# Weight forms made in a staggered order from two rings, loads ahead of stores, one normalisation piece a step

## The chip, the cores and the metric

The kernel runs on one core of a Trainium2 chip, in one launch. The metric is the device time of a run in microseconds. A core has TensorE (matmuls), VectorE, ScalarE, GpSimd, and SyncE, whose queue issues nearly all DMAs here; each engine takes its instructions in the order in which the program lists them.

## What is computed

Attention over a window of 64 positions, then a feed-forward layer with an ELU, then eight experts whose outputs are all added with gate weights that come from eight rounds of row and column normalisation:

```python
attn = softmax(q @ k^T / 8 within the window) @ v        # 4 x 8 heads x 576 x 64
x = attn as (2304, 512)
h = x @ w_in;  x = elu(h) @ w_out                        # d_ff 2048
P = exp(x @ w_gate - max)
for _ in range(8):
    P /= P.sum(1) + 1e-9;  P /= P.sum(0) + 1e-9;  P *= N / E
out = sum over e of P[:, e] * (relu(x @ w1[e]) @ w2[e])  # E 8, F 1024
```

All is float32. Products are made of three passes with operands split into a high part (rounded to the matmul format) and a low part (the rest): high x high, high x low, low x high.

## The kernel before

The stages run one after another, each keeping TensorE fed: attention with the first quarter of the feed-forward layer mixed in; the other quarters (`steps`, 20 steps each for five token blocks and four hidden chunks; four blocks of 512 tokens and one of 256); the experts for the first 768 tokens by plain products (`esteps`); the experts for the other 1536 tokens by a transformed product with seven half-size products for eight.

The seven products need sums and differences of quarters of `w1[e]` and `w2[e]`. These *forms* are made once, while the plain products of `esteps` run, and written to DRAM. There are 64 pieces, `h` = 0 to 63: expert, one of four 128-row groups, and `w1` (even) or `w2` (odd). A piece has four raw blocks of 128 x 256 and four sums of them, in eight slots. `p_tasks(h)` lists five tasks for a piece: `sums1` and `sums2` (two sums each, GpSimd), `high` (ScalarE rounds all eight slots into the tile `f`, line 666), `low` of slots 0 to 3 (VectorE, line 670), and `rest`, which makes `low` of slots 4 to 7, issues the store of seven slots and then, through `p_load(h + 2)`, four loads of 128 KB (lines 630, 635). The raw tile `rw` has eight slots and two buffers; tile `f` has eight buffers, of which 0 and 1 are in pool A1, 2 and 3 in A2 (opened at step 2 of `esteps`), 4 to 7 in B, which takes the place of the pool big1 once the gates' products are done (`done2`).

Who makes which task when is written out by hand. In the last 20 steps of the feed-forward layer the loads of pieces 0 and 1 go out at step 2, and from step 9 on each step takes one task off `ptasks`. In `esteps` each step s first lists the first product of a chunk (`e_in`), then the second product of the chunk two steps back (`e_out`), then up to two pieces of `extra`, then tasks until `ntask` reaches a goal that grows by 5 tasks for every 3 clock units (a clock unit is 256 tokens of a chunk):

```python
            clock += nb[j] // 256
            goal = 5.0 * (4.0 + clock / 3.0)
            if s >= 2:
                lim = 5 * (NHU if done2 else 4)
                while ptasks and ntask < min(goal, lim):
```

A unit of the loop is two or four chunks over 512 tokens (j = 0) and over 256 (j = 1); a full unit has 12 clock units. `e_in` takes 12 matmuls of the block's width (lines 709 to 711), `e_out` takes 12 (j = 0) or 6 (j = 1) matmuls of 512 columns (lines 727 to 729) into four or two of the four PSUM banks of tag `ac`, and `e_done` adds them into `acc` on VectorE (line 743 for the first expert, line 747 for the others). ScalarE and VectorE split the hidden values (lines 231 and 232).

`extra` holds, for each token block of the layer's result, two splits, a store, and the gates' products `gate_a` and `gate_b` (these five are also noted in `gate_fs`), and behind the last block's the eleven pieces of `sink_parts`: the maximum in two pieces (lines 546, 551, 553), `first` (exponential, row sums), seven `mid` (column sums through a product with ones, line 578; then row sums, line 574) and a last `cols`. By the order of the lists five older pieces are left when `esteps` begin, so the last `gate_b` stands in step 4, both pieces of the maximum in step 5, `first` and a `mid` in step 6, two `mid` in each of steps 7 to 9 and `cols` in step 10.

Of the kernel before, what the change touches and what calls it, by code (L numbers as in the profile page):

```python
# [8 lines left out]
F32 = mybir.dt.float32  # L9
R32 = mybir.dt.float32r  # L10
I32 = mybir.dt.int32
AF = mybir.ActivationFunctionType
ALU = mybir.AluOpType
# [5 lines left out]
def kernel(  # L19
# [14 lines left out]
    nc = tc.nc  # L34
    B, H, S, D = q.shape
# [3 lines left out]
    P = 128  # L39
# [12 lines left out]
    def r(ap):  # L52
        return ap.bitcast(F32)
# [546 lines left out]

    NP = FF // 2 // P
    HB2 = 2 * P
    SLA = {1: 0, 2: 1, 3: 6, 4: 2, 5: 3, 6: 4, 7: 5}
    SLB = {1: 0, 2: 1, 3: 2, 4: 6, 5: 3, 6: 4, 7: 5}
    PURE = [{(0, 0): 0, (0, 1): 1, (1, 1): 2, (1, 0): 7}, {(0, 0): 0, (1, 0): 1, (1, 1): 2, (0, 1): 7}]
    wd1 = [[tc.dram_tile([P, 7, 2, HB2], F32, name=f"wdi{e}_{p}") for p in range(NP)] for e in range(E)]
    wd2 = [
        [tc.dram_tile([P, 7, 2, 2, HB2], F32, name=f"wdo{e}_{pp}") for pp in range(NP // 2)]  # L610
        for e in range(E)
    ]
    NHU = E * NP * 2
    rws, forms = {}, {}
    pools = {}

    def p_at(h):
        return h // (2 * NP), h // 2 % NP, h % 2

    def p_load(h):  # L620
        if h >= NHU:
            return
        e, p, m = p_at(h)
        rw = pools["rw"].tile([P, 8, HB2], F32, tag="rw", bufs=2, name="rw")
        rws[h] = rw
        hf, hd = FF // 2, DM // 2
        for (f, d), s in PURE[m].items():
            f0 = f * hf + p * P
            if m == 0:
                nc.sync.dma_start(  # L630
                    out=rw[:, s].rearrange("p (c f) -> p c f", c=2),
                    in_=w1[e][d * hd:(d + 1) * hd, f0:f0 + P].rearrange("(c p) f -> p c f", p=P),
                )
            else:
                nc.sync.dma_start(out=rw[:, s], in_=w2[e][f0:f0 + P, d * hd:(d + 1) * hd])  # L635

    def p_tasks(h):
        e, p, m = p_at(h)

        def tt(o, a, b, op):  # L640
            rw = rws[h]
            nc.gpsimd.tensor_tensor(out=rw[:, o], in0=rw[:, a], in1=rw[:, b], op=op)  # L642

        def sums1():
            if m == 0:
                tt(3, 7, 2, ALU.add)
                tt(4, 3, 0, ALU.subtract)
            else:
                tt(3, 7, 0, ALU.subtract)
                tt(4, 3, 2, ALU.subtract)  # L650

        def sums2():
            if m == 0:
                tt(5, 0, 7, ALU.subtract)
                tt(6, 1, 4, ALU.subtract)
            else:
                tt(5, 2, 7, ALU.subtract)
                tt(6, 1, 4, ALU.add)

        def high():  # L660
            b = h % 8
            t = pools["A1" if b < 2 else "A2" if b < 4 else "B"].tile(
                [P, 8, 2, HB2], R32, tag=f"f{b}", name=f"f{b}"
            )
            forms[h] = t
            nc.scalar.activation(t[:, :, 0, :], rws[h], AF.Copy)  # L666

        def low(s):
            t = forms[h]
            nc.vector.tensor_tensor(  # L670
                out=t[:, s, 1, :], in0=rws[h][:, s], in1=r(t[:, s, 0, :]), op=ALU.subtract
            )

        def rest():
            low(slice(4, 8))
            rws.pop(h)
            to = wd1[e][p] if m == 0 else wd2[e][p // 2][:, :, p % 2]
            nc.sync.dma_start(out=to, in_=r(forms[h][:, 0:7]))
            p_load(h + 2)

        return [sums1, sums2, high, lambda: low(slice(0, 4)), rest]

    ptasks = []

# [302 lines left out]
    with tc.manual_schedule():  # L987
# [129 lines left out]
        for s, st in enumerate(steps):  # L1117
            u, j, i = st
            su = s % per_u
            if su == 0 and u + 1 < NU:  # L1120
                for kk in range(2 * UF):
                    bg += w_tasks(2 * UF * (u + 1) + kk)
            step_in(st)
            queue.append(st)
            rate = 0 if su < 3 else 5
            run_bg(rate // 2)
            while len(queue) > 2:
                moe1_out(queue.pop(0), extra)
            run_later()
            run_bg(rate - rate // 2)  # L1130
            run_later()
            run_later()
            if u == NU - 1:
                if su == 2:
                    assert not bg
                    close(wa_cm)
                    close(raw_cm)
                    open_pool("rw", "right")
                    open_pool("A1", "right")
                    p_load(0)  # L1140
                    p_load(1)
                    ptasks += p_tasks(0) + p_tasks(1)
                elif su > 8 and ptasks:
                    ptasks.pop(0)()
            if extra:
                extra.pop(0)()
# [2 lines left out]
            ("e", u, j, x)  # L1149
            for u in range(len(eunits)) for j in range(2) for x in range(len(eunits[u][1]))  # L1150
        ]
        ptasks += [f for h in range(2, NHU) for f in p_tasks(h)]

        clock = 0
        begun = 2.0
        ntask = 10
        done2 = False
        xq = []
        for s, st in enumerate(esteps):
            _, u, j, x = st  # L1160
            e_in(st)
            queue.append(st)
            while len(queue) > 2:
                q0 = queue.pop(0)
                if q0[0] != "e":
                    moe1_out(q0, extra)
                else:
                    e_out(q0)
            run_later()
            run_later()  # L1170
            if s == 2:
                close(wb_cm)
                open_pool("A2", "right")
            for _ in range(2):
                if extra:
                    extra.pop(0)()
                    run_later()
            if s >= 2 and not done2 and not any(f in gate_fs for f in extra):
                close(big1_cm)
                open_pool("B", "left")  # L1180
                done2 = True

            clock += nb[j] // 256
            goal = 5.0 * (4.0 + clock / 3.0)
            if s >= 2:
                lim = 5 * (NHU if done2 else 4)
                while ptasks and ntask < min(goal, lim):
                    ptasks.pop(0)()
                    ntask += 1
            if u == len(eunits) - 1:  # L1190
                if (j, x) == (0, 1):
                    assert not ptasks
                    for nm in ("A2", "A1", "rw"):
                        close(pools[nm + "_cm"])
                    P2["xf_cm"], P2["xf"] = pool("xf", side="right")
                    P2["w1p_cm"], P2["w1p"] = pool("w1p", side="right")
                    x_load(1)
                    for n in range(NW1):
                        w1_load(n)
                    xq += [f for fs in x_steps.values() for f in fs]  # L1200
                for _ in range(2):
                    if xq:
                        xq.pop(0)()
# [74 lines left out]
```

## Time and profile before

| | us |
|---|---|
| median of 3 runs | 2139.65 |
| lowest, highest | 2137.56, 2146.19 |
| the profiled execution | 2142.74 |
| its span, first to last instruction | 2141.0 |
| TensorE matmuls busy | 2057.9 (96%) |
| VectorE, ScalarE, GpSimd busy | 1376.4, 793.4, 684.1 |
| mean granted clock of TensorE | 0.981 of full speed |

The profile is that of one execution. Busy shares are means over stages with different limits: the stages follow each other in time, attention and the feed-forward layer to about 556 us, the plain experts with the making of forms to 1171, the transformed experts to the end. A matmul's shown duration holds its pipeline time; matmuls in a row start closer together than that.

### The profile page before, as it was taken

The numbers are of one execution on the slowest core, as the hardware profiler recorded it, in microseconds if no ns is written. First come the engines' busy times: TensorE is split into PE (matmuls) and PEld (weight loads), VectorE is DVE, ScalarE is ACT, GpSimd is POOL, SyncE is SP. The second block draws the span as 40 slices with busy tenths as digits, with TensorE's granted clock in tenths as the row PEclk, the third lists the DMA queues.
The fourth block names the chain that finished last, engine by engine and source line by source line (L and its number), as shares of the span: only waits on it lengthen the run. The fifth ranks groups of instructions, "written<-read, shape, count | busy, mean of one in ns | idle before, by whom it ended". The sixth has DMA issues, their size and how long they took to land.

```text
span 2141.0 us, 35894 instructions
## 1 busy us (share of the span) xinstructions
PE 2057.9 (96%) x13336; PEld 1877.9 (88%) x13336; DVE 1376.4 (64%) x2687; ACT 793.4 (37%) x1616; POOL 684.1 (32%) x698
## 2 busy tenths in 40 slices
PE   8999999999949899999999999999998999999998
PEld 6888888888837788878788999999998999999998
DVE  7944776844555544444545677777777777777776
ACT  5675333333422333333333433333333333333332
POOL 5532221210122333333333333333334332323322
PEclk9999999999979999999999999999999999999999
DMA  7630111101557787878776877787777877777884
GB/s 171 132 78 19 60 49 40 39 21 56 180 187 233 253 272 267 273 263 274 263 265 231 284 249 252 248 248 251 249 248 238 273 252 246 250 251 247 250 249 135
DMA packets 260349, 430.75 MB, mean 201 GB/s; under 512 B 74512, under 2 KB 138064, under 8 KB 255696
## 3 DMA queue, kind: packets, MB, share of 16 engines
q1 hardware_dynamic: 260096, 428.43, 63.2%
q8 instruction: 106, 1.74, 0.3%
q14 instruction: 67, 0.55, 0.1%
q10 hardware_dynamic: 80, 0.03, 0.0%
HBM read 302.53 MB, written 125.83 MB: 200 GB/s over the span
## 4 chain that ended last, share of the span: by engine, by line
PE 71%; DVE 8%; DMA 7%; SPq 5%; POOL 4%; ACT 3%; issue 2%; POOLq 0%; DVEq 0%; ACTq 0%
PE la L883 12%; PE ob L957 11%; PE oa L957 11%; PE lb L883 9%; DMA rw<-in_moe_w_dram 7%; POOL rw L642 4%; PE p L189 3%; SPq L635 3%; PE p L190 3%; PE p L191 3%; PE ac L491 2%; PE ac L490 2%; PE ac L489 2%; ACT f L666 2%; DVE f L670 2%
## 5 line engine op out<-in xcount | busy, mean ns | idle before, releaser
L865 POOL TENSOR_TENSOR h<-s,h 128x384 fp32r<-128x384 f32 x256 | 314.3, 1248 | 621.9 <-ACT h L856 565.7
L642 POOL TENSOR_TENSOR rw<-rw 128x256 f32<-128x256 f32 x256 | 207.1, 830 | 486.4 <-DMA rw<-in_moe_w_dram 325.9
L883 PE MATMUL la<-xf,w1f 128*128 128x384 f32 x1536 | 306.0, 337 | 9.8 <-ACT u L896 5.0
L670 DVE TENSOR_TENSOR f<-rw,f 128x1024 fp32r<-128x1024 f32 x128 | 159.4, 1257 | 222.6 <-ACT f L666 214.5
L883 PEld LDWEIGHTS la<-xf,w1f 128*128 128x128 f32 x1536 | 263.8, 189 | 11.6 <-ACT u L896 6.4
L957 PE MATMUL oa<-w2f,h 128*128 128x256 f32 x2016 | 258.9, 282 | 0.8 <-DVE acc L978 0.8
L957 PE MATMUL ob<-w2f,h 128*128 128x256 f32 x2016 | 259.3, 283 | 0.0
L957 PEld LDWEIGHTS oa<-w2f,h 128*128 128x128 f32 x2016 | 254.8, 190 | 1.0 <-DVE acc L978 1.0
L957 PEld LDWEIGHTS ob<-w2f,h 128*128 128x128 f32 x2016 | 255.0, 191 | 0.0
L861 DVE SCALAR_TENSOR_TENSOR h<-c,h 128x384 fp32r<-128x384 f32 x192 | 177.0, 922 | 102.5 <-ACT h L856 102.0
L883 PE MATMUL lb<-xf,w1f 128*128 128x384 f32 x1152 | 232.7, 336 | 0.0
L666 ACT ACTIVATE f<-rw 128x2048 fp32r<-128x2048 f32 x64 | 122.5, 1915 | 216.0 <-POOL rw L642 208.9
L883 PEld LDWEIGHTS lb<-xf,w1f 128*128 128x128 f32 x1152 | 200.9, 189 | 0.1
L709 PE MATMUL p<-xh,f 128*128 128x256 f32 (+1 forms) x512 | 176.7, 345 | 0.0
L710 PE MATMUL p<-xl,f 128*128 128x256 f32 (+1 forms) x512 | 175.7, 343 | 0.0
L856 ACT ACTIVATE h<-s 128x384 fp32r<-128x384 f32 x256 | 130.2, 523 | 121.8 <-DVE s L900 50.0
L711 PE MATMUL p<-xh,f 128*128 128x256 f32 (+1 forms) x512 | 174.8, 341 | 0.0
L727 PE MATMUL ac<-f,hh 128*128 128x512 f32 x384 | 154.2, 402 | 18.5 <-DVE acc L747 18.5
L978 DVE SCALAR_TENSOR_TENSOR acc<-oa,Pr,acc 128x256 f32<-128x256 f32 x330 | 138.7, 474 | 37.7 <-PE oa L957 37.7
L978 DVE SCALAR_TENSOR_TENSOR acc<-ob,Pr,acc 128x256 f32<-128x256 f32 x318 | 133.7, 474 | 34.4 <-PE ob L957 34.3
L856 ACT ACTIVATE h<-c 128x384 fp32r<-128x384 f32 x192 | 100.4, 523 | 147.0 <-DVE c L891 104.4
L728 PE MATMUL ac<-f,hh 128*128 128x512 f32 x384 | 153.1, 399 | 0.0
(143 smaller groups left out, 3701.7 us busy)
## 6 DMA issues: line engine op xcount, KB each, us to landing
w1f<-wdi SPq DMA_DIRECT2D x448, 256.0 KB, 3.8
w2f<-wdo SPq DMA_DIRECT2D x224, 512.0 KB, 4.1
wdi<-f SPq DMA_DIRECT2D x32, 1792.0 KB, 6.8
wdo<-f SPq DMA_DIRECT2D x32, 1792.0 KB, 7.4
rw<-in_moe_w_dram SPq DMA_DIRECT2D x256, 128.0 KB, 6.7
raw<-in_moe_w_in_dram SPq DMA_DIRECT2D x16, 512.0 KB, 4.0
raw<-in_moe_w_out_dram SPq DMA_DIRECT2D x16, 512.0 KB, 3.6
qn<-in_q_dram SPq DMA_DIRECT2D x32, 144.0 KB, 3.9
```

The lines of the kernel that those rows point to most:

```text
L642: nc.gpsimd.tensor_tensor(out=rw[:, o], in0=rw[:, a], in1=rw[:, b], op=op)
L666: nc.scalar.activation(t[:, :, 0, :], rws[h], AF.Copy)
L670: nc.vector.tensor_tensor(out=t[:, s, 1, :], in0=rws[h][:, s], in1=r(t[:, s, 0, :]), op=ALU.subtract)
L709: nc.tensor.matmul(p1[:, :n], w[:, s, 0, cs], xh, start=(c == 0), stop=False)
L710: nc.tensor.matmul(p1[:, :n], w[:, s, 0, cs], xl, start=False, stop=False)
L711: nc.tensor.matmul(p1[:, :n], w[:, s, 1, cs], xh, start=False, stop=(c == NCC - 1))
L856: nc.scalar.activation(h[:, 0], src, AF.Relu if relu else AF.Copy)
L861: nc.vector.scalar_tensor_tensor(h[:, 1], src, 0.0, r(h[:, 0]), op0=ALU.max, op1=ALU.subtract)
L865: nc.gpsimd.tensor_tensor(out=h[:, 1], in0=src, in1=r(h[:, 0]), op=ALU.subtract)
L883: nc.tensor.matmul(o, w[:, a, c, :], x[:, b, c, :], start=first and c == 0 and z == 0, stop=last and c == 1 and z == 2, skip_group_check=True,
L957: nc.tensor.matmul(o[:, c * HB2:(c + 1) * HB2], hs[p][:, a, c * P:(c + 1) * P], w[:, p, b, :], start=fresh and c != 1 and p == 0 and z == ...
L978: nc.vector.scalar_tensor_tensor(a, src, pe, a, op0=ALU.mult, op1=ALU.add)
```

## The change

`rw` becomes a ring of three raw tiles of four slots, and the sums go to a ring of their own, `sw`, with two tiles of four slots; the raw quarter that stood in slot 7 now stands in slot 3, the sums in 4 to 7, of which, as before, seven slots in all are stored, now by two DMAs. ScalarE and VectorE take raw blocks and sums one after the other (`part` 0 and 1). The tasks are staggered: the second halves and the store of piece h - 1 are made within the tasks of piece h, and `p_load(h + 3)` is listed after the raw half of h. Three loads go out at first and three tasks more are queued in the feed-forward layer's last steps, with `ntask` starting at 13 and the limit before `done2` raised by 3. `extra` gives two pieces a step only while one of the gates' products is left in it, one a step after that.

```diff
@@ -600,18 +600,19 @@
 
 
 
+
     NP = FF // 2 // P
     HB2 = 2 * P
     SLA = {1: 0, 2: 1, 3: 6, 4: 2, 5: 3, 6: 4, 7: 5}
     SLB = {1: 0, 2: 1, 3: 2, 4: 6, 5: 3, 6: 4, 7: 5}
-    PURE = [{(0, 0): 0, (0, 1): 1, (1, 1): 2, (1, 0): 7}, {(0, 0): 0, (1, 0): 1, (1, 1): 2, (0, 1): 7}]
+    PURE = [{(0, 0): 0, (0, 1): 1, (1, 1): 2, (1, 0): 3}, {(0, 0): 0, (1, 0): 1, (1, 1): 2, (0, 1): 3}]
     wd1 = [[tc.dram_tile([P, 7, 2, HB2], F32, name=f"wdi{e}_{p}") for p in range(NP)] for e in range(E)]
     wd2 = [
         [tc.dram_tile([P, 7, 2, 2, HB2], F32, name=f"wdo{e}_{pp}") for pp in range(NP // 2)]
         for e in range(E)
     ]
     NHU = E * NP * 2
-    rws, forms = {}, {}
+    rws, sws, forms = {}, {}, {}
     pools = {}
 
     def p_at(h):
@@ -621,7 +622,7 @@
         if h >= NHU:
             return
         e, p, m = p_at(h)
-        rw = pools["rw"].tile([P, 8, HB2], F32, tag="rw", bufs=2, name="rw")
+        rw = pools["rw"].tile([P, 4, HB2], F32, tag="rw", bufs=3, name="rw")
         rws[h] = rw
         hf, hd = FF // 2, DM // 2
         for (f, d), s in PURE[m].items():
@@ -634,51 +635,81 @@
             else:
                 nc.sync.dma_start(out=rw[:, s], in_=w2[e][f0:f0 + P, d * hd:(d + 1) * hd])
 
-    def p_tasks(h):
-        e, p, m = p_at(h)
+    def p_sums(h, part):
+        rw = rws[h]
+        if part == 0:
+            sws[h] = pools["rw"].tile([P, 4, HB2], F32, tag="sw", bufs=2, name="sw")
+        sw = sws[h]
 
         def tt(o, a, b, op):
-            rw = rws[h]
-            nc.gpsimd.tensor_tensor(out=rw[:, o], in0=rw[:, a], in1=rw[:, b], op=op)
-
-        def sums1():
-            if m == 0:
-                tt(3, 7, 2, ALU.add)
-                tt(4, 3, 0, ALU.subtract)
-            else:
-                tt(3, 7, 0, ALU.subtract)
-                tt(4, 3, 2, ALU.subtract)
-
-        def sums2():
-            if m == 0:
-                tt(5, 0, 7, ALU.subtract)
-                tt(6, 1, 4, ALU.subtract)
-            else:
-                tt(5, 2, 7, ALU.subtract)
-                tt(6, 1, 4, ALU.add)
-
-        def high():
+            nc.gpsimd.tensor_tensor(out=sw[:, o], in0=a, in1=b, op=op)
+
+        x11, x12, x22, x21 = [rw[:, s] for s in range(4)]
+        if h % 2:
+            x12, x21 = x21, x12
+        if h % 2 == 0 and part == 0:
+            tt(0, x21, x22, ALU.add)
+            tt(1, sw[:, 0], x11, ALU.subtract)
+        elif h % 2 == 0:
+            tt(2, x11, x21, ALU.subtract)
+            tt(3, x12, sw[:, 1], ALU.subtract)
+        elif part == 0:
+            tt(0, x12, x11, ALU.subtract)
+            tt(1, sw[:, 0], x22, ALU.subtract)
+        else:
+            tt(2, x22, x12, ALU.subtract)
+            tt(3, x21, sw[:, 1], ALU.add)
+
+    def p_high(h, part):
+        if part == 0:
             b = h % 8
-            t = pools["A1" if b < 2 else "A2" if b < 4 else "B"].tile(
+            forms[h] = pools["A1" if b < 2 else "A2" if b < 4 else "B"].tile(
                 [P, 8, 2, HB2], R32, tag=f"f{b}", name=f"f{b}"
             )
-            forms[h] = t
-            nc.scalar.activation(t[:, :, 0, :], rws[h], AF.Copy)
-
-        def low(s):
-            t = forms[h]
-            nc.vector.tensor_tensor(
-                out=t[:, s, 1, :], in0=rws[h][:, s], in1=r(t[:, s, 0, :]), op=ALU.subtract
-            )
-
-        def rest():
-            low(slice(4, 8))
-            rws.pop(h)
-            to = wd1[e][p] if m == 0 else wd2[e][p // 2][:, :, p % 2]
-            nc.sync.dma_start(out=to, in_=r(forms[h][:, 0:7]))
-            p_load(h + 2)
-
-        return [sums1, sums2, high, lambda: low(slice(0, 4)), rest]
+        src = (rws if part == 0 else sws)[h]
+        nc.scalar.activation(forms[h][:, 4 * part:4 * part + 4, 0, :], src, AF.Copy)
+
+    def p_low(h, part):
+        t = forms[h][:, 4 * part:4 * part + 4]
+        src = (rws if part == 0 else sws).pop(h)
+        nc.vector.tensor_tensor(out=t[:, :, 1, :], in0=src, in1=r(t[:, :, 0, :]), op=ALU.subtract)
+
+    def p_store(h):
+        e, p, m = p_at(h)
+        to = wd1[e][p] if m == 0 else wd2[e][p // 2][:, :, p % 2]
+        nc.sync.dma_start(out=to[:, 0:3], in_=r(forms[h][:, 0:3]))
+        nc.sync.dma_start(out=to[:, 3:7], in_=r(forms[h][:, 4:8]))
+
+
+
+    def p_tasks(h):
+        def begin():
+            p_sums(h, 0)
+
+        def sums():
+            p_sums(h, 1)
+            if h:
+                p_high(h - 1, 1)
+
+        def lows():
+            if h:
+                p_low(h - 1, 1)
+
+        def highs():
+            p_high(h, 0)
+            if h:
+                p_store(h - 1)
+
+        def last():
+            p_low(h, 0)
+            p_load(h + 3)
+
+        def end():
+            p_high(h, 1)
+            p_low(h, 1)
+            p_store(h)
+
+        return [begin, sums, lows, highs, last] + ([end] if h == NHU - 1 else [])
 
     ptasks = []
 
@@ -1137,9 +1168,9 @@
                     close(raw_cm)
                     open_pool("rw", "right")
                     open_pool("A1", "right")
-                    p_load(0)
-                    p_load(1)
-                    ptasks += p_tasks(0) + p_tasks(1)
+                    for h in range(3):
+                        p_load(h)
+                    ptasks += p_tasks(0) + p_tasks(1) + p_tasks(2)[:3]
                 elif su > 8 and ptasks:
                     ptasks.pop(0)()
             if extra:
@@ -1149,11 +1180,10 @@
             ("e", u, j, x)
             for u in range(len(eunits)) for j in range(2) for x in range(len(eunits[u][1]))
         ]
-        ptasks += [f for h in range(2, NHU) for f in p_tasks(h)]
+        ptasks += [f for h in range(2, NHU) for f in p_tasks(h)][3:]
 
         clock = 0
-        begun = 2.0
-        ntask = 10
+        ntask = 13
         done2 = False
         xq = []
         for s, st in enumerate(esteps):
@@ -1171,7 +1201,7 @@
             if s == 2:
                 close(wb_cm)
                 open_pool("A2", "right")
-            for _ in range(2):
+            for _ in range(2 if any(f in gate_fs for f in extra) else 1):
                 if extra:
                     extra.pop(0)()
                     run_later()
@@ -1183,7 +1213,7 @@
             clock += nb[j] // 256
             goal = 5.0 * (4.0 + clock / 3.0)
             if s >= 2:
-                lim = 5 * (NHU if done2 else 4)
+                lim = 5 * (NHU if done2 else 4) + 3
                 while ptasks and ntask < min(goal, lim):
                     ptasks.pop(0)()
                     ntask += 1
```

## Rows read from the trace of the kernel before

**Rows 1.** The page's 40 slices, TensorE: busy tenths.

```profile
PE   8999999999949899999999999999998999999998
```

**Rows 2.** Windows: each engine busy, granted clock, DMA share, GB/s.

```profile
core 0: us, PE busy (x) PEld busy (x) DVE busy (x) ACT busy (x) POOL busy (x), PEclk, DMA share, GB/s
580.00:590.00 10.00, 6.20 (x32) 4.78 (x30) 2.23 (x5) 1.91 (x1) 3.11 (x5) 0.95 1.01 352
600.00:610.00 10.00, 2.67 (x12) 2.27 (x13) 3.49 (x5) 3.37 (x4) 5.93 (x8) 0.50 0.62 214
...
659.67:1172.00 512.33, 493.86 (x2456) 416.02 (x2455) 257.37 (x324) 160.38 (x177) 188.20 (x223) 0.99 0.78 263
```

**Rows 3.** TensorE's waits from 560 us: total us, times, longest us.

```profile
PE mxT L551 <- DVE mx L546: 20.6, 1, 20.6
PE ac L727 <- DVE acc L747: 18.5, 12, 3.5
PE csum L578 <- DVE cs L574: 14.7, 4, 5.5
```

**Rows 4.** TensorE's timeline: start us, us, line, form [idle before <- releaser].

```profile
607.33 0.58 PE L551 MATMUL mxT<-ident,mx 128*1 128x128 f32 x2 [20.62 <-DVE mx L546]
...
654.00 0.29 PE L578 MATMUL csum<-cs,ones 128*128 128x8 f32 x2
...
768.03 0.28 PE L709 MATMUL p<-xh,f 128*128 128x256 f32 x1
...
769.43 0.39 PE L727 MATMUL ac<-f,hh 128*128 128x512 f32 x1
...
772.23 0.28 PE L709 MATMUL p<-xh,f 128*128 128x256 f32 x1
...
1170.88 1.21 PE L883 MATMUL la<-xf,w1f 128*128 128x384 f32 x6
```

**Rows 5.** Timelines in the dip: VectorE, ScalarE, GpSimd, SyncE's queue.

```profile
582.36 0.17 DVE L534 COPY Lg<-lt 128x16 f32<-128x16 f32 x1 [0.70 <-PE lt L531]
...
605.15 1.22 DVE L670 TENSOR_TENSOR f<-rw,f 128x1024 fp32r<-128x1024 f32 x1 [7.31 <-ACT f L666]
...
606.89 0.29 DVE L546 TENSOR_REDUCE mx<-Lg 128x1 f32<-128x144 f32 x1
...
603.21 1.91 ACT L666 ACTIVATE f<-rw 128x2048 fp32r<-128x2048 f32 x1 [7.77 <-POOL rw L642]
...
600.29 2.89 POOL L642 TENSOR_TENSOR rw<-rw 128x256 f32<-128x256 f32 x4 [6.79 <-DMA rw<-in_moe_w_dram]
...
591.62 0.32 SPq L678 DMA_DIRECT2D wdi<-f  x1
592.04 4.21 SPq L630 DMA_DIRECT2D rw<-in_moe_w_dram  x4
597.90 0.53 SPq L678 DMA_DIRECT2D wdo<-f  x1
```

**Rows 6.** Waits of the whole trace: total us, times, longest us.

```profile
POOL rw L642 <- DMA rw<-in_moe_w_dram: 325.9, 53, 19.5
...
DVE f L670 <- ACT f L666: 214.5, 55, 9.0
...
ACT f L666 <- POOL rw L642: 208.9, 55, 9.2
```

**Rows 7.** DMA issues, raw blocks: count, KB each, median us to landing.

```profile
rw<-in_moe_w_dram SPq DMA_DIRECT2D x256, 128.0 KB, 6.7
```

**Rows 8.** VectorE's timeline: first and last instruction of two normalisation rounds.

```profile
617.61 0.17 DVE L580 TENSOR_SCALAR rc<-csum 128x8 f32<-128x8 f32 x1 [0.48 <-PE csum L578]
...
620.58 0.44 DVE L574 TENSOR_REDUCE cs<-Pr 128x8 f32<-128x144 f32 x1
...
628.12 0.17 DVE L580 TENSOR_SCALAR rc<-csum 128x8 f32<-128x8 f32 x1 [0.69 <-PE csum L578]
...
630.30 0.42 DVE L574 TENSOR_REDUCE cs<-Pr 128x8 f32<-128x144 f32 x1
```

**Rows 9.** GpSimd's timeline: the last x forms of the next stage.

```profile
1160.02 3.66 POOL L798 TENSOR_TENSOR xf<-xb,xf 128x768 fp32r<-128x768 f32 x2
```

## The prediction

> **What bounds the kernel now.** I read the slices of the page first, then the windows around the dip, then the waits of TensorE, then the timelines of each engine inside the dip.
>
> In the slices [rows 1] TensorE is at 8 or 9 tenths everywhere but for one stretch around slice 12 of 40, about 590 to 650 us. All of the change acts from the last pass of the first feed-forward stage (about 510 us) to the start of the transformed stage at 1170.88 us [rows 4]; what stands before and behind that I leave as it is. So the question is how much of TensorE's time between 580 and 1171 us is not work. TensorE's waits from 560 us on [rows 3] name three that matter: 20.6 us once at `mxT` (first product of the normalisation, waits for VectorE's maximum), 14.7 us at `csum` (column sums, wait for VectorE's row sums), 18.5 us in 12 pieces at line 727 (a PSUM bank that VectorE's line 747 has not yet emptied).
>
> *The dip.* TensorE's last matmul before it ended at 586.71 us (607.33 less the 20.62 idle), and the last of the normalisation's column sums starts at 654.00 [rows 4]: 67.3 us. The steps in between (s = 6 to 10 of the expert loop, by the code's order) hold 24 matmuls of 256 columns and 84 of 512. Their full-speed pitch I take from a quiet stretch: twelve of 256 from 768.03 to 769.43 are 0.117 us each, twelve of 512 from 769.43 to 772.23 are 0.233 us [rows 4]. That is 2.8 + 19.6 = 22.4 us, and about 2 us for nine small products: 24.5 us of work in 67.3. **42.8 us are lost in the dip.** Idle time is 35.3 us of it (20.6 + 14.7); the rest is matmuls run after an idle stretch, when the granted clock is at its lower level: 0.50 (1.2 GHz) in 600 to 610 us [rows 2].
>
> *Why it is idle.* In the trace the maximum `mx` (606.89) stands on VectorE's queue behind five low parts of form pieces; the last of them began at 605.15 after 7.31 us of waiting for ScalarE, whose 1.91 us rounding at 603.21 had waited 7.77 us for GpSimd, whose sums at 600.29 had waited 6.79 us for raw blocks [rows 5]. On SyncE's queue the four loads of those blocks left at 592.04, right behind the store at 591.62 [rows 5], which in the program must wait for VectorE's low parts of the piece before. So it is a loop through four engines: store, load, sums, high, low, store, with two buffers. In the whole trace GpSimd waits 325.9 us for loads, ScalarE 208.9 for sums, VectorE 214.5 for ScalarE [rows 6].
>
> *The steady stage.* From 659.67 to 1170.88 us are 511.2 us. A full unit of the loop is 120 matmuls of 512 and 48 of 256: 28.0 + 5.6 = 33.6 us. There are 14 of them, and 16.8 us left of the third unit (48 of each size): 487.2 us. **24.0 us are lost**: 18.5 at line 727 [rows 3], some 5.5 at the lower clock behind the longest of these waits (mean 0.99 [rows 2]). DMA is busy 0.78 of it, at 263 GB/s [rows 2]. VectorE is busy 257 us of 512, so it is late because it waits in its queue, not because it is full.
>
> **The change part by part.**
>
> *Loads ahead, rings of three and two.* A load now leaves 11 tasks before the sums of its block (before: 6), and stands on SyncE's queue ahead of the store that shares its turn. Twenty tasks go with 12 clock units, 33.6 us, so 11 are 18 us, and 10 tasks in the four quickest steps (13.9 us) still make 15. The need: 4.2 us to issue four loads [rows 5], 6.7 us median from issue to landing [rows 7]: 11 us. Before, 6 tasks were 10 us, less than the need; that is the 6 to 7 us wait on each piece. I take it as gone. Raw blocks are rounded without any sum: the matmuls of this stage use only slots 0 to 3.
>
> *High and low parts in halves.* ScalarE makes two of 128x1024 in place of one of 128x2048 (1.91 us [rows 5]); that form is not in the trace. It costs no less than half (0.96) and no more than the whole; near half, so +0.1 to 0.2 us a piece, on an engine busy 160 of the steady stage's 512 us [rows 2]: nothing. VectorE's two halves and GpSimd's four sums stay as they are in number and shape.
>
> *Store in two.* One more issue a piece, 0.32 to 0.53 us [rows 5]; SyncE goes from about 4.8 to 5.2 us of 8.4 a piece: covered. Bytes are the same: 0.52 MB in, 1.84 MB out.
>
> *Later forms.* `high` of the raw half moves from third task to fourth and its `low` from fourth to fifth, and the counter starts at 13 where only 11 of the 13 queued tasks find a step (steps 9 to 19). Together three tasks, 5 us later. The lead of the tightest form over its first matmul falls from some 21 us to 16, against a chain of about 1 + 1.2 us: covered.
>
> *The burst at step 4.* Eleven tasks now go at once there, before 14. They need blocks 5 and 6; 4 has been in for long, 5 and 6 are asked for at step 2, some 10 us earlier. VectorE has four low parts of 1.2 us in front of `mx`, whose data are there, so from its last gate copy (582.36 [rows 5]) `mx` can be had by about 590. And `mxT` stands one step later on TensorE, behind 4.2 us of matmuls: at about 590.9. So the 20.6 us fall to 0 to 3.
>
> *One normalisation piece a step.* The chain runs over steps 5 to 15 instead of 5 to 10; its result is first read at step 21. One round is 2.6 us on VectorE, 628.12 to 630.72 [rows 8], and about 0.7 through TensorE. Before, two in a step had 4.2 us of matmuls between pairs and nothing within one. Now each has a whole step. But VectorE is nearly full there. Steps 8 to 14: TensorE 4.2 + 4.2 + 5.6 + 5.6 + 4.2 + 4.2 + 2.8 = 30.8 us; VectorE seven rounds at 3.0 (between 2.6 and 3.4, below) = 21, hidden low parts 4.0, PSUM sums 3.8, some 7.6 form halves at 1.22 = 9.3: 38 us. The excess of 7 to 8 us remains as waits at `csum`. So of the dip's 42.8 us about 35 go.
>
> A round measured 3.4 us (617.61 to 621.02) where GpSimd's sums ran beside it and 2.6 where none did [rows 8]. The Trainium skill (SBUF — State Buffer, Who interferes with whom) says that a VectorE instruction with two SBUF inputs and a GpSimd instruction that reads SBUF exclude each other for a whole instruction. By that rule rounds now spread among GpSimd's sums would all take the longer time, 24 us in place of 21, and the dip give 32 instead of 35; without it, 38.
>
> *The end of the stage.* The last piece's three tasks go one step later (about 4 us), so do the x loads behind it. The last x form is done at 1163.7 [rows 9], 7.2 us before the next stage needs any: covered.
>
> **The sum**: 35 in the dip, 22 of 24 in the steady stage (2 left, for TensorE's own starts): 57 us. Profiled time 2142.74 - 57 = 2085.7. That execution lies 3.1 us above the median of the three runs (2139.65), which would give 2082.6; I say 2085.
>
> **The rivals.**
> - *The dip goes, the steady waits stay* (14%). Line 727's waits come from VectorE's order; if a first half of a piece still holds it up, only 35 us come: 2105 to 2108. For: VectorE still has the same 128 low parts ahead of line 747. Against: 214.5 us of its waits hang on the loads.
> - *VectorE binds the normalisation* (14%). One round a step costs as much as before if form halves and rounds pile up: 20.6 of the dip and 22 come, 2097 to 2100.
> - *The forms come late* (6%). TensorE has no wait at lines 709 to 711 now; three tasks' delay could make one. It decides from 16 us on. At 3 us a unit and a clock drop behind each, 14 units take back 45 to 60: 2130 to 2143, no change.
> - *Slower: DMA becomes the bound of the stage* (6%). Loads before stores and stores in two shorter runs could lower the rate. A unit moves 9.44 MB; 33.6 us want 281 GB/s. Below 246 GB/s a unit takes 38.4 us, 70 us more over 14.5 units, which outweighs 57: 2150 and more. For: 263 GB/s at a share of 0.78 is the mean. Against: 352 GB/s at a share of 1.01 in 580 to 590 us [rows 2], and 263/0.78 = 337.
>
> The forecast itself (2072 to 2097) has 58%; 2% is for what I don't see.
>
> **How the numbers follow.** All losses gone would be 66.8 us: 2139.65 - 66.8 = 2073, and a us or two for the run's spread: 2071. Upwards the range takes in the first two rivals and leaves out the last two: 2112. A difference of 0.5% (10.7 us) is what this measurement can tell from none. Faster by more: 58 + 14 + 14 and a share of the rest, 0.88; within it 0.06; slower 0.06.
>
> **What would show it.** GpSimd's wait for raw blocks and VectorE's for line 666's successor fall to a small part; TensorE has no 20 us wait at `mxT`; waits at line 727's successor under 4 us; a few waits of 1 to 3 us at `csum` until about 640 us, and the transformed stage starting near 1114. It is wrong if TensorE waits for a form tile, if DMA stands at 1.0 over many slices, or if the stage from the dip to the transformed one takes over 560 us.

## The result and the profile after

The changed kernel takes **2081.23 us** (median of 4 runs, 2080.76 to 2082.14) against 2141.61 of the kernel before measured beside it (2137.56 to 2146.19): a ratio of 0.9718, 95% interval 0.9696 to 0.9740. Forecast were 2085 us and a range of 2071 to 2112. Of the runs behind this document one of the kernel before (4036 us) and one of number 12 (5101 us) were far slower than all others; the ratios leave them out, and number 12's median is that of its other three. The profiled execution took 2082.14 us with a span of 2080.1, 60.9 less than before.

The slices of the page, TensorE's busy tenths, to be held against [rows 1]: the dip is gone.

```profile
PE   8999999999999999999999999999998999999998
```

Where the 60.9 us came from is read off three marks in TensorE's timeline: the last gate product (line 531), the start of step 16 of the expert loop, where the normalisation is over in both kernels, and the first product of the transformed stage. Before:

```profile
581.72 0.61 PE L531 MATMUL lt<-sel,lgT 16*128 16x8 f32 x4 [0.50 <-DVE lgT L522]
...
673.68 0.39 PE L709 MATMUL p<-xh,f 128*128 128x512 f32 x1
```

and with 1170.88 [rows 4] as the third. After (start us, us, line, form, idle before it):

```profile
580.71 0.61 PE L531 MATMUL lt<-sel,lgT 16*128 16x8 f32 x4 [0.50 <-DVE lgT L522]
...
590.71 0.50 PE L758 MATMUL ac<-f,hh 128*128 128x512 f32 x1 [2.21 <-ACT acc L772]
...
593.25 0.58 PE L551 MATMUL mxT<-ident,mx 128*1 128x128 f32 x2
...
639.23 0.47 PE L740 MATMUL p<-xh,f 128*128 128x512 f32 x1
...
1109.68 1.21 PE L914 MATMUL la<-xf,w1f 128*128 128x384 f32 x6
```

From the first mark to the second: 92.0 us before, 58.5 after: 33.4 won in the dip. From the second to the third: 497.2 and 470.5: 26.8 won in the steady stage. The first mark is 1.0 us earlier, and the rest of the run 0.3 longer. `mxT`, which waited 20.62 us [rows 4], has no wait now; the one wait ahead of it is 2.21 us at a PSUM bank that ScalarE had to empty. ScalarE came late to it because a rounding ahead of it waited for GpSimd's sums:

```profile
588.63 1.06 ACT L670 ACTIVATE f<-sw 128x1024 fp32r<-128x1024 f32 x1 [4.25 <-POOL sw L645]
...
590.07 1.08 ACT L772 ACTIVATE acc<-ac 128x512 f32<-128x512 f32 x2
```

TensorE's waits from 555 us on (total us, times, longest) that stand where [rows 3] stood, without those of the transformed stage:

```profile
PE csum L578 <- DVE cs L574: 3.2, 2, 2.6
...
PE ac L758 <- ACT acc L772: 2.2, 1, 2.2
```

The 14.7 us at `csum` are 3.2, and line 778, which takes the place of line 747, makes TensorE wait no more. The windows say the same (columns as in [rows 2]; the last window is the steady stage, 14 units):

```profile
core 0: us, PE busy (x) PEld busy (x) DVE busy (x) ACT busy (x) POOL busy (x), PEclk, DMA share, GB/s
580.00:590.00 10.00, 8.00 (x42) 6.34 (x40) 6.35 (x6) 4.34 (x5) 8.68 (x9) 1.00 1.04 355
600.00:610.00 10.00, 10.00 (x47) 8.19 (x46) 9.41 (x22) 4.04 (x5) 2.93 (x4) 1.00 0.97 375
639.23:1109.68 470.45, 470.12 (x2368) 397.00 (x2366) 261.15 (x318) 160.72 (x225) 187.27 (x215) 1.00 0.77 279
```

TensorE is busy 470.1 of 470.45 us, at the full clock (1.00), with the DMA engines at 0.77. VectorE has as much work as before (261 us). In 600 to 610 us, where the clock stood at 0.50 in [rows 2], it is 1.00; the lower level is not gone from the dip, though: behind the 2.21 us wait the mean of 590 to 600 us is 0.83.

Who waits for whom in the making of forms (whole trace), in place of [rows 6]:

```profile
POOL sw L645 <- DMA rw<-in_moe_w_dram: 44.2, 5, 16.2
...
DVE f L675 <- ACT f L670: 6.6, 27, 0.3
```

GpSimd's 325.9 us for raw blocks are 44.2, VectorE's 214.5 for ScalarE are 6.6, ScalarE's 208.9 for sums are a single wait of 4.3. GpSimd is not idle for less time: 203.9 us of its waits at line 645 now have no releaser that the profile shows, and 68.9 are for VectorE's line 675. The DMA issues of raw blocks (KB each, median us to landing), in place of [rows 7]:

```profile
rw<-in_moe_w_dram SPq DMA_DIRECT2D x256, 128.0 KB, 2.8
```

2.8 us in place of 6.7, with the same size and count. And SyncE's queue in the steady stage:

```profile
769.24 1.77 SPq L636 DMA_DIRECT2D rw<-in_moe_w_dram  x4
771.05 0.43 SPq L680 DMA_DIRECT2D wdi<-f  x1
773.58 0.33 SPq L681 DMA_DIRECT2D wdi<-f  x1
```

Four loads take 1.77 us to issue where they took 4.21 right behind a store [rows 5]. This pair of readings I had not foreseen, and the experiments begin with it.

Two normalisation rounds on VectorE, first and last instruction, in place of [rows 8]:

```profile
603.41 0.17 DVE L580 TENSOR_SCALAR rc<-csum 128x8 f32<-128x8 f32 x1
...
606.44 0.48 DVE L574 TENSOR_REDUCE cs<-Pr 128x8 f32<-128x144 f32 x1
...
625.41 0.15 DVE L580 TENSOR_SCALAR rc<-csum 128x8 f32<-128x8 f32 x1
...
627.58 0.42 DVE L574 TENSOR_REDUCE cs<-Pr 128x8 f32<-128x144 f32 x1
```

The first, with GpSimd's sums beside it, is 3.5 us long (603.41 to 606.92), the second, without, 2.6 (625.41 to 628.00). The last x form, for [rows 9]:

```profile
1100.28 3.66 POOL L829 TENSOR_TENSOR xf<-xb,xf 128x768 fp32r<-128x768 f32 x2
```

It ends at 1103.94, 5.7 us before the transformed stage: covered, as forecast.

### The profile page after: what moved, and what is told of

It reads as the page before. It is cut to its first block, busy times and chain, and to the rows that moved or that the text cites. A ratio compares the mean times of both kernels' runs of the same rounds, so it can differ in the third digit from the quotient of the medians.

```text
span 2080.1 us, 35944 instructions
## 1 busy us (share of the span) xinstructions
PE 2042.9 (98%) x13336; PEld 1866.0 (90%) x13336; DVE 1387.5 (67%) x2687; ACT 797.7 (38%) x1680; POOL 691.8 (33%) x698
## 4 chain that ended last, share of the span: by engine, by line
PE 84%; DVE 6%; issue 6%; DMA 1%; POOL 1%; ACT 1%; SPq 0%; DVEq 0%; POOLq 0%; ACTq 0%
PE la L914 13%; PE ob L988 11%; PE oa L988 11%; PE lb L914 9%; PE ac L760 4%; PE ac L759 4%; PE ac L758 4%; PE p L740 4%; PE p L741 4%; PE p L742 4%; PE p L189 3%; PE p L191 2%; PE p L190 2%; PE ac L491 2%; PE ac L490 2%
## 5 line engine op out<-in xcount | busy, mean ns | idle before, releaser
L645 POOL TENSOR_TENSOR sw<-rw 128x256 f32<-128x256 f32 x128 | 123.7, 967 | 407.1 <-issue 203.9
L232 DVE SCALAR_TENSOR_TENSOR hl<-p,hh 128x256 fp32r<-128x256 f32 (+1 forms) x128 | 71.1, 556 | 201.3 <-ACT hh L231 201.2
L231 ACT ACTIVATE hh<-p 128x256 fp32r<-128x256 f32 (+1 forms) x128 | 62.8, 490 | 336.1 <-PE p L742 331.2
L740 PE MATMUL p<-xh,f 128*128 128x256 f32 (+1 forms) x512 | 174.0, 340 | 0.0
L742 PE MATMUL p<-xh,f 128*128 128x256 f32 (+1 forms) x512 | 172.5, 337 | 0.0
L758 PE MATMUL ac<-f,hh 128*128 128x512 f32 x384 | 151.9, 396 | 2.2 <-ACT acc L772 2.2
L760 PE MATMUL ac<-f,hl 128*128 128x512 f32 x384 | 151.7, 395 | 0.3 <-DVE hl L232 0.3
```

Source lines behind the costliest of these rows:

```text
L645: nc.gpsimd.tensor_tensor(out=sw[:, o], in0=a, in1=b, op=op)
L740: nc.tensor.matmul(p1[:, :n], w[:, s, 0, cs], xh, start=(c == 0), stop=False)
L742: nc.tensor.matmul(p1[:, :n], w[:, s, 1, cs], xh, start=False, stop=(c == NCC - 1))
L758: nc.tensor.matmul(o, gh[:, tcs], wh, start=(x == 0), stop=False)
L760: nc.tensor.matmul(o, gl[:, tcs], wh, start=False, stop=l)
```

## The experiments

The kernel before was timed beside each group. Ratios are to it, with 95% intervals.

| | us | ratio |
|---|---|---|
| changed kernel | 2081.23 | 0.9718 (0.9696 to 0.9740) |
| 1 two pieces a step again | 2098.43 | 0.9795 (0.9779 to 0.9812) |
| 2 only one piece a step | 2127.74 | 0.9933 (0.9918 to 0.9947) |
| 3 loads right behind stores | 2084.20 | 0.9728 (0.9713 to 0.9742) |
| 4 two raw buffers | 2084.16 | 0.9730 (0.9716 to 0.9745) |
| 5 not staggered | 2080.44 | 0.9707 (0.9689 to 0.9724) |
| 6 stagger, latest loads | 2094.16 | 0.9773 (0.9757 to 0.9789) |
| 7 early loads, old tasks | 2086.70 | 0.9739 (0.9720 to 0.9758) |
| 8 forms later | 2136.22 | 0.9972 (0.9961 to 0.9982) |
| 9 a third more traffic | 2083.86 | 0.9721 (0.9707 to 0.9736) |
| 10 burst spread, round shorter | 2074.22 | 0.9679 (0.9662 to 0.9695) |
| 11 order alone | 2089.89 | 0.9755 (0.9736 to 0.9773) |
| 12 burst spread | 2076.64 | 0.9689 (0.9670 to 0.9708) |

The ratios of numbers 3, 4, 5, 7 and 9 lie inside the changed kernel's interval. Their times alone do not tell them from it; what is said of differences of 3 us rests on the waits.

**1. Two pieces a step again**, the rest as changed.

```diff
-            for _ in range(2 if any(f in gate_fs for f in extra) else 1):
+            for _ in range(2):
```

> The changed kernel with two pieces of the normalisation a step again, all else as changed. If pairs of rounds expose TensorE (my reading of the dip): the maximum's product waits about 5 us again (585.5 to 590.8 us), the column sums wait some 15 us in all as before, and half-clock matmuls behind the longer waits cost another 4 to 8: 2096 to 2108 us. Rival: VectorE's work is the bound of the stretch whichever way it is split, so waits only move: 2081 to 2086 us.

Measured 2098.43 us, 17.2 more. TensorE's waits in its expert loop:

```profile
PE csum L578 <- DVE cs L574: 12.8, 4, 3.7
PE mxT L551 <- DVE mx L546: 5.5, 1, 5.5
```

As expected for pairs of rounds that expose TensorE: 5.5 us at `mxT`, 12.8 at `csum`, 12.9 us more idle than the changed kernel's 5.4, the rest behind them. The rival, that VectorE's load alone sets this stretch, falls.

**2. Only one piece a step**: that line in the kernel before.

```diff
-            for _ in range(2):
+            for _ in range(2 if any(f in gate_fs for f in extra) else 1):
```

> The kernel before with one piece a step and nothing else of the change. If the two parts of the gain are separate: mxT's wait falls only by the 4.2 us of matmuls now ahead of it (20.6 to about 16), the column sums' 14.7 us fall to 3 or so with some clock behind them, line 727's 18.5 us stay: 2113 to 2128 us. Rival: low parts stuck on loads stand between the rounds on VectorE's queue and keep the column sums waiting: 2133 us or more.

Measured 2127.74 us: 14 us of the change's 60.

```profile
PE ac L727 <- ACT acc L741: 16.1, 1, 16.1
PE ac L727 <- DVE acc L747: 15.0, 11, 3.8
PE csum L578 <- DVE cs L574: 7.4, 4, 3.0
```

Both readings hold half: `csum` fell from 14.7 to 7.4, not to 3, since low parts that wait for loads still stand between the rounds; the 20.6 us of `mxT` became 16.1 us at a PSUM bank in front of it, and line 747's waits stayed (15.0 against 18.5).

**11. Order alone** (run last, told here since it answers number 2): number 2, and the loads of piece h + 2 ahead of the store of h. Two buffers, six tasks of lead and whole pieces stay.

```diff
             rws.pop(h)
+            p_load(h + 2)
...
-            p_load(h + 2)
```

> The kernel before with one normalisation piece a step and a single move: the loads of piece h + 2 issued ahead of the store of h (two raw tiles, six tasks of lead, old tasks). Against 2127.74 us with the one-piece part alone. If order alone empties the loop: landing near 2.8 us, line 727's 15 us under 4 and some clock, 2095 to 2108 us with the burst still hurting. If a second remedy is needed with whole pieces: line 727 keeps 10 us or more, 2115 to 2127 us.

Measured 2089.89 us, better than the better of the two expectations: 38 us from one moved call. Its waits of TensorE, its raw loads in the DMA issues, SyncE's queue, and a window of the steady stage (columns as above) in number 2 and here:

```profile
PE ac L727 <- ACT acc L741: 10.5, 1, 10.5
PE csum L578 <- DVE cs L574: 4.4, 4, 3.0
...
PE ac L727 <- DVE acc L743: 0.2, 1, 0.2
```

```profile
rw<-in_moe_w_dram SPq DMA_DIRECT2D x256, 128.0 KB, 2.7
```

```profile
760.95 1.92 SPq L630 DMA_DIRECT2D rw<-in_moe_w_dram  x4
762.91 0.47 SPq L679 DMA_DIRECT2D wdi<-f  x1
```

```profile
660.00:1070.00 410.00, 395.79 (x1941) 332.44 (x1940) 207.33 (x260) 129.43 (x138) 145.56 (x182) 0.98 0.80 267
```

```profile
660.00:1070.00 410.00, 410.00 (x2061) 346.20 (x2060) 228.55 (x275) 139.00 (x148) 173.36 (x196) 1.00 0.77 284
```

Line 747 makes TensorE wait no more at all (18.5 us [rows 3]; 0.2 are left at line 743). Landing is 2.7 us and four issues 1.92. TensorE is busy the whole 410 us of the window, at the full clock. Six tasks are enough if the loads don't stand behind a store. GpSimd's wait for loads did not fall with it: 348.1 us, against 308.1 in number 2, and TensorE sees none of it. What is left against the changed kernel is the burst: 10.5 us at one PSUM bank.

**3. Loads right behind stores** in the changed kernel, 7 tasks ahead of the sums.

```diff
                 p_store(h - 1)
+                p_load(h + 2)
...
             p_low(h, 0)
-            p_load(h + 3)
```

> The changed kernel with each piece's loads issued behind the store of the piece whose buffer they take (7 tasks ahead of their sums in place of 11). Theory order (a load that stands behind a 1.84 MB store pays 4.2 us of issue and 6.7 to land): issue per load back to about 1 us, landing back to 6 us or more, 11 us against 10 to 12 us of lead, TensorE waits at the PSUM banks again in part: 2088 to 2100 us. Theory stagger (raw halves need no sums, and sums have five tasks of slack): landing times rise but nothing waits: 2081 to 2084 us.

Measured 2084.20 us. Issue per load doubled (0.92 us, was 0.46), landing rose and GpSimd waits 33 times:

```profile
rw<-in_moe_w_dram SPq DMA_DIRECT2D x256, 128.0 KB, 4.7
```

```profile
POOL sw L645 <- DMA rw<-in_moe_w_dram: 99.3, 33, 16.6
```

The one wait of TensorE that grew stands in the burst: 5.5 us in place of 2.2. In the steady stage it waits for none of it. The theory of order has the mechanism right and the time wrong here.

**4. Two raw buffers**, loads six tasks ahead but not behind a store.

```diff
-        rw = pools["rw"].tile([P, 4, HB2], F32, tag="rw", bufs=3, name="rw")
+        rw = pools["rw"].tile([P, 4, HB2], F32, tag="rw", bufs=2, name="rw")
...
-            p_load(h + 3)
+            p_load(h + 2)
...
-                    for h in range(3):
+                    for h in range(2):
```

> The changed kernel with two raw buffers and loads 6 tasks ahead, as many as before the change, but still ahead of the store. Theory lead (the number of tasks ahead is what counts): GpSimd waits for loads again, 15 to 22 us come back: 2096 to 2103 us. Theory order: a load takes 1.9 us to issue and 2.8 to land, 5 us against 10 of lead, nothing waits: 2081 to 2084 us.

Measured 2084.16 us: the theory that the number of tasks ahead counts falls. Landing is 2.6 us. The wait that grew is again the one at the burst's bank, 4.7 us in place of 2.2.

**5. Not staggered**: rings and early loads stay, both halves of a piece are made in its own five tasks. The last three of them, and their order, then read (`begin` and `sums` only make sums):

```python
        def highs():
            p_high(h, 0)
            p_high(h, 1)
...
        def lows():
            p_low(h, 0)
            p_load(h + 3)
...
        def last():
            p_low(h, 1)
            p_store(h)
...
        return [begin, sums, highs, lows, last]
```

> The changed kernel with each piece's five tasks in the old order (sums, sums, both highs, raw low and the load, sum low and the store): rings of three and two and loads ahead of stores stay, the stagger goes. Theory stagger (VectorE stays on time because it never meets a low part whose sums are fresh): waits on line 675 and at the PSUM banks come back, 2092 to 2105 us. Theory either (with loads 11 tasks ahead the sums are ready early anyhow, so one remedy is enough): 2081 to 2086 us.

Measured 2080.44 us, the changed kernel's time. Beside loads that leave early and ahead of the store, the stagger buys nothing.

**6. The stagger with the latest loads**: two buffers, loads behind the store and two tasks ahead.

```diff
-        rw = pools["rw"].tile([P, 4, HB2], F32, tag="rw", bufs=3, name="rw")
+        rw = pools["rw"].tile([P, 4, HB2], F32, tag="rw", bufs=2, name="rw")
...
                 p_store(h - 1)
+                p_load(h + 1)
...
             p_low(h, 0)
-            p_load(h + 3)
...
-                    for h in range(3):
+                    for h in range(2):
```

> The changed kernel with two raw buffers and each piece's loads behind the store of the piece two before, only 2 tasks ahead of their first sums: stagger alone, with loads later than before the change. Theory stagger: raw halves are still five tasks behind the load, about 8 us against 5 to 11 of need, VectorE is seldom late: 2083 to 2092 us. Theory either (neither remedy alone survives late loads): VectorE waits for raw blocks on each piece, PSUM banks come late: 2100 us or more.

Measured 2094.16 us, just above the one expectation and below the other; the trace decides. TensorE's waits, and the window of its steady stage:

```profile
PE ac L758 <- ACT acc L772: 10.4, 2, 7.3
...
PE ac L758 <- DVE acc L774: 0.3, 1, 0.3
```

```profile
core 0: us, PE busy (x) PEld busy (x) DVE busy (x) ACT busy (x) POOL busy (x), PEclk, DMA share, GB/s
653.00:1124.00 471.00, 470.29 (x2366) 397.41 (x2367) 267.93 (x319) 164.25 (x225) 207.91 (x216) 1.00 0.81 280
```

The steady stage is as quick as the changed kernel's (470.3 us of TensorE in 471.0), though GpSimd waits 240.6 us for loads in this run. The 13 us stand in the burst and just ahead of it, 10.4 us of them at the banks that ScalarE empties, behind roundings that wait for raw blocks. So in the steady stage the stagger, with its rings and halves, is enough by itself. With number 5: neither it nor the early load ahead of the store is needed beside the other.

**7. Early loads, old tasks**: number 2 with three raw tiles of eight slots and the loads of h + 3 ahead of the store of h.

```diff
-        rw = pools["rw"].tile([P, 8, HB2], F32, tag="rw", bufs=2, name="rw")
+        rw = pools["rw"].tile([P, 8, HB2], F32, tag="rw", bufs=3, name="rw")
...
             rws.pop(h)
+            p_load(h + 3)
...
-            p_load(h + 2)
...
                     p_load(1)
+                    p_load(2)
```

> The kernel before with one normalisation piece a step, three raw tiles of eight slots, and the loads of piece h + 3 issued ahead of the store of h; tasks, forms and store as before. Against 2127.74 us with the one-piece part alone. If early loads are enough (theory either): GpSimd's waits for blocks go from 308 to under 80 us, line 727's from 15 to under 3, the burst's 16 us shrink to 5: 2084 to 2095 us. If the stagger is what counts: waits at line 727 stay near 15 us, 2105 us or more.

Measured 2086.70 us, within 6 of the changed kernel. As expected for early loads, line 747 causes no wait; the expected fall of GpSimd's wait for blocks did not come (293.6 us). GpSimd has little but the sums to do in this stage; done with one piece, it waits for the blocks of the next, and TensorE does not feel it here or in number 11. That number is no sign of harm by itself.

**8. Forms later** by eight tasks from step 8 on.

```diff
-                while ptasks and ntask < min(goal, lim):
+                late = 8 if 8 <= s and u < len(eunits) - 1 else 0
+                while ptasks and ntask < min(goal - late, lim):
```

> The changed kernel with every task from step 8 of the expert loop on 8 tasks (about 13 us) later against the matmuls. I worked out a lead of 16 us for the tightest form. If that is right, TensorE still has no wait at the first products: 2081 to 2084 us. If the forms were already near their due time (the rival of late forms), TensorE waits at lines 740 to 742 in each unit: 2095 us or more.

Measured 2136.22 us: the rival's outcome. TensorE's wait, and the window over the steady stage (columns as above):

```profile
PE p L742 <- DVE f L675: 27.5, 13, 3.5
```

```profile
640.00:1165.00 525.00, 491.48 (x2355) 408.70 (x2355) 258.74 (x318) 163.70 (x228) 208.57 (x223) 0.96 0.71 258
```

Once a unit, 13 times, it waits about 2 us for a low part, at the third pass, the first that reads it, and the mean clock of the stage is 0.96 in place of 1.00: 55 us in all, half of them idle. My lead of 16 us was an average pace. Tasks are taken step by step, and the form's lead runs over the four quick steps, 13.9 us for ten tasks: eight tasks later it is made in the very step before its use, and on VectorE behind an `e_done`. Between 0 and 8 tasks was not tried.

**9. A third more traffic**: slots 0 to 2 stored twice.

```diff
+    more = [tc.dram_tile([P, 3, 2, HB2], F32, name=f"more{z}") for z in range(8)]
...
+        nc.sync.dma_start(out=more[h % 8], in_=r(forms[h][:, 0:3]))
```

> The changed kernel with slots 0 to 2 of every piece stored a second time, to a spare tensor: 0.79 MB more a piece, 2.36 to 3.15 MB, a third more traffic in the expert loop. If the transfer engines have the room that the busiest windows show (375 to 397 GB/s in 590 to 610 us), a unit's 12.6 MB take 33.5 us at best, as long as its matmuls: 2081 to 2115 us at a share near 1. If the mean rate over its share (337 GB/s) is the ceiling, 37.3 us a unit and 52 more over 14 units: about 2133 us.

Measured 2083.86 us, 2.6 more. The page's DMA lines (busy tenths, GB/s):

```profile
DMA  7631111110399999999997778788787878778874
...
GB/s 168 132 86 25 51 51 41 51 31 21 127 371 398 386 397 370 382 368 386 382 361 273 246 250 251 248 249 252 248 255 230 281 248 248 251 248 248 253 248 132
```

The transfer engines carry 361 to 398 GB/s in ten slices of the expert loop, at 9 tenths, and the line in the place of line 747 still causes no wait of TensorE. The ceilings I took in the prediction (337, 352) are too low for this mix: a third more traffic fits. How much more fits was not tried.

**10 and 12. A faster version?** In number 10 the tasks of step 4's burst are spread over steps 4 to 18 and the factor N/E joins the product; number 12 has the first of these alone.

```diff
+                if done2:
+                    lim = min(lim, 28 + 3 * (s - 4) if s < 8 else 37 + 2 * (s - 7) if s < 15 else 51 + 4 * (s - 14))
...
-            nc.vector.tensor_scalar(rc, rc, float(NT) / E, None, op0=ALU.mult)
-            nc.vector.tensor_tensor(
-                out=Pr, in0=Pr, in1=rc.unsqueeze(1).to_broadcast([P, NTT, E]), op=ALU.mult
-            )
+            nc.vector.scalar_tensor_tensor(
+                Pr, Pr, float(NT) / E, rc.unsqueeze(1).to_broadcast([P, NTT, E]),
+                op0=ALU.mult, op1=ALU.mult,
+            )
```

> An attempt at a faster version: the changed kernel with the burst of eleven tasks at step 4 spread over steps 4 to 18 (three, then two, then four tasks a step) and one VectorE instruction less in each normalisation round (the factor N/E joins the product). In the changed kernel 2.2 us of wait behind the burst, 3.2 at the column sums and some half-clock matmuls behind them are left, 9.7 us over work in the dip. If the burst and the rounds cause them: 2074 to 2079 us. If VectorE is full there whatever the order: 2080 to 2083 us.

> The kernel of the tenth experiment without its shorter normalisation round: only the burst of tasks at step 4 is spread. If the burst carried that experiment's gain of 7 us: 2073 to 2077 us. If the shorter round did: 2079 to 2082 us.

2074.22 and 2076.64 us. The wait behind the burst is gone in both, and the windows 580 to 640 us of the changed kernel and of number 10 show it:

```profile
580.00:640.00 60.00, 54.07 (x264) 44.02 (x262) 50.58 (x111) 19.97 (x28) 25.55 (x31) 0.94 0.88 321
```

```profile
580.00:640.00 60.00, 57.72 (x298) 48.09 (x297) 48.99 (x106) 20.72 (x30) 26.04 (x29) 1.00 0.77 284
```

57.7 us of TensorE at clock 1.00 in place of 54.1 at 0.94. Most of the 7 us is the spread; the 2.4 us between the two versions are inside their runs' scatter. Number 10's interval lies just below the changed kernel's, number 12's overlaps it. Number 10 is the fastest of this study.

## Why the prediction was right, and where its steps were not

- *The dip* (42.8 us lost, 35 to come back): right, 33.4 came. `mx` was forecast for about 590 us and `mxT` unhindered at 590.9; they came at 590.81 and 593.25, the latter behind the 2.21 us at a PSUM bank, which was not forecast. That `mx` fell on the forecast time is in part luck: VectorE's four low parts took 1.21 to 1.76 us each, not 1.2, and it then waited 2.90 us for ScalarE. Forecast to stay were 7 to 8 us of waits at `csum`. Of the 58.5 us between the first two marks 48.8 are work by the prediction's own pitches (162 matmuls of 512 columns, 72 of 256 and the small ones), so 9.7 stayed: 3.2 at `csum`, 2.2 at the bank, and the rest mostly matmuls at the lower clock. Number 2 shows that the burst's loads, not the normalisation, held the first 16 us; number 1 shows the price of pairs, 17 us.
- *Rounds at 3.0 us on a VectorE nearly full*: of seven rounds three took 3.5 to 3.7 us and four 2.6, 21.1 us in all against 21 forecast. VectorE's timeline lists no wait from 599.84 to 639.41 us, so it was full, as reckoned. By the Trainium skill's rule (SBUF — State Buffer, Who interferes with whom) all would have taken the longer time only if GpSimd's sums had run beside each; they ran beside three. Where they did, the trace agrees with the rule that each blocks the other (rows in the last section).
- *The steady stage* (24.0 us lost, 22 to come back): right in kind; the term was undersized. The changed kernel does the 14 units in 470.45 us, which is the work I had counted (470.4), so nothing is left of it, and the loss before was 26.8 us. The 24.0 came of a miscount: the rest of the third unit, 659.67 to 673.68 us, holds 36 matmuls of 512 columns and not 48, 14.0 us of work and not 16.8, and nothing was lost in it.
- *Loads ahead*: the outcome was right, the cause was not, and that the forecast came out is luck in this step. I held 6 tasks (10 us) against a need of 11 us (4.2 to issue, 6.7 to land) and let 11 tasks cure it; that the loads would now stand ahead of the store I named, and gave no price. The need itself was made by the place right behind a 1.84 MB store: elsewhere it is 1.8 + 2.8 = 4.6 us. Moving one call ahead of the store, with six tasks of lead, won 38 us (number 11). For the steady stage the place ahead of the store suffices alone (number 11) and so does the stagger (number 6). In the changed kernel none of early issue, place and stagger is needed beside the other two, which is why undoing one of them costs 3 us or nothing (numbers 3 to 5). Early issue alone, behind the store and without the stagger, was not run.
- *Later forms*: three tasks later cost nothing, as forecast, but the lead was less than I said (number 8).
- *The rivals*: line 747's waits did not stay, VectorE, though full, cost TensorE 3.2 us at the rounds and not the 14 us of that rival, and DMA had room (number 9). Late forms are real, at eight tasks more, and there they cost the 45 to 60 us that the rival gave (55).

That a load behind a store lands late since its pieces queue behind the store's on the transfer engines fits the rows and was not measured by itself; issue and landing times are what is shown.

## What to carry to other kernels

Before counting how far ahead a load is issued, look at what stands right in front of it on its queue: a load behind a large store costs issue time and landing time here, and moving it is one line. When a change holds several remedies, undo them one at a time and also do each alone: here two of them were each enough alone, so undoing either would have called it worthless. Work of a small serial chain goes between large pieces one link a step, and a lead counted in tasks is worth what the steps that take them are long.

## What the hardware showed that was not expected

- A load of 128 KB takes 0.43 to 0.46 us to issue and 2.8 us to land (median of 256), 1.02 to 1.13 and 6.7 right behind a store of 1.84 MB.
- VectorE's low part and GpSimd's sums lengthen one another. Rows of the changed kernel, VectorE alone and twice with GpSimd beside it, then GpSimd beside VectorE and alone:

```profile
606.82 1.23 DVE L675 TENSOR_TENSOR f<-rw,f 128x1024 fp32r<-128x1024 f32 x1
...
573.75 1.77 DVE L675 TENSOR_TENSOR f<-sw,f 128x1024 fp32r<-128x1024 f32 x1
575.43 1.76 DVE L675 TENSOR_TENSOR f<-rw,f 128x1024 fp32r<-128x1024 f32 x1
...
574.51 1.60 POOL L645 TENSOR_TENSOR sw<-sw,rw 128x256 f32<-128x256 f32 x1
576.07 1.72 POOL L645 TENSOR_TENSOR sw<-rw 128x256 f32<-128x256 f32 x1
...
596.15 0.74 POOL L645 TENSOR_TENSOR sw<-rw 128x256 f32<-128x256 f32 x1
```

VectorE takes 1.23 us alone and 1.76 beside sums, GpSimd 0.74 alone and 1.60 to 1.72. A turn of the two takes 1.7 us (573.75 to 575.43). Alone, low parts in a row start 1.14 us apart and sums 0.70, together 1.84: side by side they save a tenth of that.
- The transfer engines moved up to 398 GB/s in a slice of 52 us (number 9).
